# Linear attention beside softmax attention on one core: A's Q and K are copied out of PSUM before phi is made, and the engines' orders are planned anew

## The chip, the core and the metric

The kernel runs on one core of a Trainium2 chip. The core has five engines with a queue of instructions each: TensorE (PE, with its weight loads shown apart as PEld), VectorE (DVE), ScalarE (ACT), GpSimd (POOL) and SyncE (SP), which here only issues DMAs. An engine works its queue in order; where an instruction needs another engine's result it waits for a semaphore, and all that stands behind it on that engine waits too. The metric is the device time of one execution in microseconds (us).

## The reference

Two attention blocks of the same shape are computed on separate inputs and set side by side. S is 2048, D is 512, 32 heads of 16; inputs are bfloat16.

```python
def A(x, wqkv, wo):                      # linear attention
    q, k, v = heads(x @ wqkv)
    phi = lambda t: where(t > 0, t + 1, exp(t)) + 1e-6
    pq, pk = phi(q), phi(k)
    kv = einsum("bhsd,bhse->bhde", pk, v)
    z = sum over s of pk
    o = (pq @ kv) / (pq @ z + 1e-6)
    return merge(o) @ wo

def B(x, wqkv, wo):                      # softmax attention
    q, k, v = heads(x @ wqkv)
    p = softmax(q @ k^T * 16 ** -0.5)
    return merge(p @ v) @ wo

return concatenate([A, B], axis=-1)
```

## The kernel before

B is the large part. It is cut into 32 units: four groups of eight heads, four chunks of 512 query positions, and a parity (even or odd heads of the group). A unit has 64 score blocks of 128 keys x 512 queries, so there are 2048 blocks. A block is a matmul of `QT` and `KM` (line 862), an exponential, and a matmul with the values `VV` into the accumulator `pPV` (line 1106).

The exponential is made in one of two ways:

- **The ACT path.** PE writes three or two blocks at once into one of the score buffers `pS` (1536 or 1024 columns, in turn), and ACT makes exp of them in one instruction (`PT`, line 1031). Such a block has one value matmul.
- **The DVE path.** PE writes one block into one of the two banks of `pD`; DVE turns it into the bits of an approximate exponential (`DI`, line 943); POOL adds two constants to two blocks' bits at once (line 967), which gives two shifted copies. Such a block has three value matmuls.

All other products of the kernel go through the same two banks of `pD` (`DBANK`) while the score buffers are in use: B's projections, a check of the scores' size, and all of A. The A jobs are, in order: `akv_job` (for each of four column groups and eight pairs of token tiles: K and V of two tiles side by side in one bank), `akvsum_job` (phi(K)^T V), and then for each of four chunks of positions `aq_job` (Q, one bank of 512 columns, for each of four column groups), `aden_job`, `anum_job` and `omm_job`.

phi is made of three steps, written in `phi_stages`: exp on ACT into `EA` (line 692), then min with 1 plus 1e-6 on DVE in `EA` (line 693), then max(x, 0) + `EA` on DVE into `KNa` or `PQT` (line 695). The first and third read the `pD` bank, so the bank of a K/V job is held through exp, both DVE steps and V's copy to `VNa` (line 707).

The order of each engine's instructions is decided when the program is built. A planner keeps a clock per engine (`T`) and costs per operation, picks at each step one of the instructions that could start next by start time and priority, and records it with its waits in `Sched`. A job is a list of stages `(engine, cost, function)`; `rel` is the stage after which its bank is free. The table `POLICY` has one row of planner settings for each 8 us of planned time (`SEG`): priorities, thresholds, a random seed. `TEND` spreads the due times of the A and B jobs, and `DEND` is the number of blocks at the end of the last unit that are left to the ACT path alone.

An entry "PORT" in the list of what an operation writes is a token between DVE and POOL: the POOL shift and POOL's share of a unit's end name it, and so do those DVE instructions that read and write SBUF in a fast form. Through it each waits for the other by semaphores.

```python
push(eng, end + lat, 0 if i + 1 <= self.rel and self.bank else min(self.prio, 2), dur, ...)
```

is how the next stage of a job is queued: stages up to the bank's release go with the highest priority.

Of the kernel before, what the change touches and what calls it, by code (L numbers as in the profile page):

```python
# [232 lines left out]
def bass_concat_heads__linear_attn_block__softmax_full_mha__prompt_kernel(nc, A_x, A_wqkv, A_wo, B_x, B_wqkv, B_wo, out):  # L233
# [15 lines left out]
    DEND = 20  # L249
    TEND = 720.0  # L250
    TRACE = None
    NAMES = ('DEFER', 'FLOW', 'DPR', 'DDEL', 'PVR', 'PVMIN', 'PVURG', 'DBL', 'DLEAD', 'DNEXT', 'ALAG', 'SLK', 'PA', 'PB', 'SEED', 'PARTS')
    SEG = 8.0
    POLICY = [
        (0.15, 3.5, 4.2, 0, 3, 4, 32, 3.0, 1.0, 16, 10.0, 0.0, 0, 0, 0, 1),
        (0.15, 3.5, 4.2, 0, 3, 5, 32, 3.0, 1.0, 16, 10.0, 0.0, 0, 0, 201, 1),
        (0.15, 3.5, 4.2, 0.2, 3, 4, 20, 3.0, 1.0, 16, 10.0, 0.0, 0, 0, 845, 1),
        (0.35, 4.5, 2.6, 0, 3, 4, 32, 3.0, 1.0, 16, 10.0, 0.0, 0, 0, 236, 1),
        (0.35, 2.05, 4.2, 0, 3, 5, 32, 3.0, 1.0, 16, 40.0, 0.0, 0, 0, 989, 1),
        (0.15, 3.5, 4.2, 0.2, 3, 7, 20, 3.0, 1.0, 16, 10.0, 0.0, 0, 0, 845, 1),  # L260
        (0.35, 2.5, 2.6, 0, 3, 4, 32, 3.0, 1.0, 16, 10.0, 0.0, 0, 0, 24, 1),
        (0.35, 2.5, 2.6, 0, 3, 7, 32, 3.0, 1.0, 16, 10.0, 0.0, 0, 0, 222, 1),
        (0.15, 3.5, 4.2, 0.2, 3, 5, 12, 3.0, 1.0, 16, 10.0, 0.0, 0, 0, 326, 1),
        (0.15, 3.5, 3, 0, 3, 4, 32, 3.0, 0.5, 16, 10.0, 0.0, 0, 0, 0, 1),
        (0.15, 3.5, 3, 0.3, 3, 4, 32, 3.0, 0.5, 16, 10.0, 0.0, 0, 0, 0, 2),
        (0.15, 3.5, 3, 0.3, 2, 4, 32, 3.0, 0.5, 16, 10.0, 0.0, 3, 0, 0, 2),
        (0.15, 3.5, 3, 0, 3, 4, 32, 3.0, 1.0, 16, 10.0, 0.0, 0, 0, 301, 1),
        (0.15, 3.5, 4.2, 0, 3, 6, 32, 3.0, 1.0, 16, 10.0, 0.0, 0, 0, 314, 1),
        (0.5, 3.5, 3, 0, 3, 4, 20, 3.0, 1.0, 16, 10.0, 0.0, 0, 0, 95, 2),
        (0.15, 2.05, 3, 0, 3, 4, 32, 3.0, 1.0, 24, 10.0, 0.0, 0, 0, 681, 1),  # L270
        (0.5, 3.5, 3, 0, 3, 4, 20, 3.0, 1.0, 16, 10.0, 0.0, 0, 0, 430, 2),
        (0.15, 2.5, 3, 0, 3, 4, 32, 3.0, 1.0, 8, 10.0, 0.0, 0, 0, 287, 1),
        (0.15, 2.05, 3, 0, 4, 5, 32, 3.0, 1.0, 24, 10.0, 0.0, 1.5, 0, 42, 1),
        (0.5, 3.5, 3, 0, 2, 4, 20, 3.0, 1.0, 16, 10.0, 0.0, 0, 0, 430, 2),
        (0.5, 3.5, 3, 0, 2, 4, 20, 3.0, 1.0, 16, 10.0, 0.0, 0, 0, 430, 2),
        (0.15, 3.5, 3, 0, 2, 5, 24, 3.0, 1.0, 24, 10.0, 0.0, 1.5, 0, 42, 1),
        (0.15, 3.5, 4.2, 0, 3, 4, 32, 3.0, 1.0, 16, 40.0, 0.05, 0, 0, 715, 1),
        (0.35, 3.5, 3, 0, 2, 5, 24, 3.0, 0.5, 24, 10.0, 0.0, 1.5, 0, 432, 1),
        (0.15, 2.5, 4.2, 0, 3, 4, 32, 9.0, 1.0, 16, 10.0, 0.0, 0, 0, 584, 1),
        (0.15, 2.5, 4.2, 0, 3, 4, 32, 9.0, 1.0, 16, 10.0, 0.0, 0, 0, 584, 1),  # L280
        (0.35, 3.5, 3, 0, 2, 8, 24, 3.0, 0.5, 24, 10.0, 0.0, 1.5, 0, 333, 1),
        (0.15, 2.5, 4.2, 0, 3, 7, 32, 9.0, 0.5, 16, 10.0, 0.0, 0, 0, 516, 1),
        (0.15, 3.5, 4.2, 0, 3, 4, 32, 3.0, 1.0, 8, 10.0, 0.0, 0, 0, 224, 1),
        (0.15, 2.05, 4.2, 0, 3, 8, 32, 3.0, 1.0, 8, 10.0, 0.0, 0, 0, 578, 1),
        (0.25, 3.5, 4.2, 0, 3, 4, 32, 3.0, 1.0, 8, 10.0, 0.0, 0, 3, 224, 1),
        (0.15, 3.5, 4.2, 0, 2, 4, 32, 3.0, 1.0, 8, 10.0, 0.0, 0, 0, 224, 1),
        (0.25, 3.5, 4.2, 0, 3, 4, 32, 3.0, 1.0, 8, 10.0, 0.0, 0, 0.5, 893, 1),
        (0.15, 2.05, 4.2, 0, 2, 4, 32, 3.0, 1.0, 8, 10.0, 0.0, 0, 0, 224, 1),
        (0.25, 3.5, 4.2, 0, 4, 4, 32, 3.0, 1.0, 8, 10.0, 0.0, 0, 0.5, 479, 1),
        (0.15, 3.5, 4.2, 0, 3, 4, 32, 3.0, 1.0, 16, 10.0, 0.0, 0, 0, 550, 1),  # L290
        (0.25, 3.5, 4.2, 0, 4, 4, 32, 3.0, 1.0, 8, 10.0, 0.1, 3, 0.5, 215, 1),
        (0.15, 3.5, 4.2, 0.2, 3, 4, 20, 3.0, 1.0, 16, 10.0, 0.0, 0, 0, 550, 1),
        (0.15, 3.5, 4.2, 0, 3, 6, 32, 3.0, 1.0, 8, 40.0, 0.0, 0, 0, 550, 1),
        (0.15, 3.5, 2.6, 0, 3, 4, 32, 3.0, 1.0, 16, 10.0, 0.0, 1.5, 0, 414, 1),
        (0.15, 2.5, 2.6, 0, 3, 4, 32, 3.0, 1.0, 16, 10.0, 0.0, 1.5, 0, 111, 1),
        (0.15, 2.5, 3, 0, 3, 4, 32, 3.0, 0.2, 16, 10.0, 0.0, 1.5, 0, 111, 1),
        (0.15, 2.5, 2.6, 0, 4, 4, 32, 3.0, 1.0, 16, 10.0, 0.0, 1.5, 0, 111, 4),
        (0.15, 2.5, 2.6, 0, 3, 4, 32, 3.0, 1.0, 16, 20.0, 0.0, 3, 3, 368, 1),
        (0.15, 2.5, 3, 0, 2, 5, 32, 3.0, 1.0, 16, 20.0, 0.0, 3, 3, 530, 1),
        (0.15, 3.5, 4.2, 0, 2, 4, 32, 3.0, 1.0, 16, 10.0, 0.0, 0, 0, 0, 1),  # L300
        (0.15, 2.5, 2.6, 0, 3, 4, 32, 3.0, 0.5, 8, 20.0, 0.0, 3, 3, 771, 1),
        (0.15, 2.5, 3, 0.3, 2, 5, 32, 6.0, 1.0, 16, 20.0, 0.0, 3, 3, 348, 4),
        (0.15, 4.5, 4.2, 0, 2, 4, 32, 3.0, 1.0, 8, 10.0, 0.0, 0, 0, 83, 1),
        (0.35, 4.5, 4.2, 0, 4, 4, 32, 3.0, 1.0, 8, 10.0, 0.0, 0, 0, 46, 1),
        (0.15, 3.5, 4.2, 0, 3, 4, 32, 3.0, 1.0, 16, 10.0, 0.0, 0.5, 0, 3, 1),
        (0.15, 4.5, 4.2, 0, 2, 4, 32, 3.0, 1.0, 8, 10.0, 0.0, 0, 0, 73, 1),
        (0.35, 2.05, 4.2, 0, 2, 4, 32, 3.0, 1.0, 8, 10.0, 0.0, 0, 0, 46, 1),
        (0.35, 2.05, 4.2, 0, 2, 4, 32, 3.0, 1.0, 8, 10.0, 0.1, 0, 1.5, 46, 1),
        (0.15, 4.5, 4.2, 0, 2, 4, 32, 3.0, 1.0, 8, 10.0, 0.0, 0, 0, 96, 2),
        (0.15, 4.5, 2.6, 0, 2, 4, 32, 3.0, 1.0, 8, 10.0, 0.0, 0, 0, 96, 2),  # L310
        (0.35, 2.05, 4.2, 0, 2, 4, 32, 3.0, 1.0, 8, 10.0, 0.1, 0, 1.5, 511, 2),
        (0.15, 3.5, 4.2, 0, 3, 8, 16, 3.0, 1.0, 8, 10.0, 0.0, 0, 0, 0, 1),
        (0.15, 3.5, 4.2, 0, 3, 4, 32, 3.0, 1.0, 16, 40.0, 0.0, 0, 0, 673, 1),
        (0.35, 2.05, 4.2, 0, 2, 5, 32, 3.0, 1.0, 8, 10.0, 0.1, 0, 1.5, 651, 2),
        (0.15, 3.5, 4.2, 0.3, 3, 4, 16, 3.0, 1.0, 16, 20.0, 0.0, 0, 0, 0, 1),
        (0.15, 3.5, 4.2, 0, 3, 4, 32, 3.0, 1.0, 16, 20.0, 0.0, 0, 0, 330, 4),
        (0.15, 3.5, 4.2, 0.3, 3, 4, 16, 3.0, 1.0, 16, 20.0, 0.0, 0, 3, 0, 2),
        (0.15, 3.5, 4.2, 0.3, 3, 4, 16, 3.0, 1.0, 16, 20.0, 0.05, 0, 3, 0, 2),
        (0.15, 3.5, 4.2, 0, 3, 4, 32, 3.0, 1.0, 16, 20.0, 0.0, 0.5, 0, 935, 4),
        (0.15, 3.5, 4.2, 0.3, 3, 4, 32, 3.0, 0.2, 16, 20.0, 0.0, 0, 0, 0, 2),  # L320
# [1126 lines left out]
```

## Time and profile before

| | |
|---|---|
| runs shown | 714.42 us median of 3 (711.8 to 714.48) |
| profiled execution | 714.82 us; span from first to last instruction 713.1 us |
| mean granted TensorE clock | 0.994 |
| ACT busy | 691.8 us (97%) |
| PE busy | 672.3 us (94%) |
| POOL busy | 559.2 us (78%) |
| DVE busy | 537.0 us (75%) |
| exponentials on ACT (`PT`) | 591, 680.1 us busy |
| DVE conversions (`DI`) | 570, 377.2 us busy |
| POOL shifts (`DI`) | 286, 534.3 us busy |
| phi's exp on ACT (`EA`) | 48, 26.9 us busy |

The span leaves out 1.7 us that lie around it. Busy times are unions of an engine's records; durations of single records overlap on ACT, DVE and PE, since the next instruction starts before the record of the last one ends. Groups of the trace carry a line of the kernel, the engine, the operation, the tile written and the tiles read with their shapes, then the busy time and mean duration of one, and after the bar the idle time of the engine in front of them with what ended it. A row of the waits gives who waited for whom, the total, how often, and the longest. A window gives the busy time of PE, PEld, DVE, ACT and POOL in a stretch.

### The profile page before, as it was taken

Reading aid. Unit: us, or ns where it says so; the run is one execution under the profiler, and the core shown is the slowest. Engines: PE = TensorE matmul, PEld = TensorE weight load, DVE = VectorE, ACT = ScalarE, POOL = GpSimd, SP = SyncE. Lnnn points to the kernel's source line nnn. Section 1 sums busy time; section 2 is a strip of 40 time slices with the busy share of each in tenths; the row PEclk is TensorE's granted clock in tenths of the full one; section 3 lists DMA queues with packets and bytes.
Section 4 is the critical chain, followed back from the end, with each engine's and each line's share of the span. In section 5 each row is a group of like instructions: output and inputs, shape, how many; then the busy total and the mean of one; then the engine's idle time right before and its main releaser. Section 6 shows DMA issues by size and latency. Waiting matters only on the chain.

```text
span 713.1 us, 15692 instructions
## 1 busy us (share of the span) xinstructions
PE 672.3 (94%) x6691; PEld 223.7 (31%) x6691; DVE 537.0 (75%) x950; ACT 691.8 (97%) x646; POOL 559.2 (78%) x338
## 2 busy tenths in 40 slices
PE   8999999999999999999999999999999999999995
PEld 4324443333333333332222223232222222222221
DVE  4778886777767877777888778888678877878771
ACT  5999999999999999999999999999999999999995
POOL 4597577677978787877899979988678987888991
PEclk9999999999899999999999999999999999999999
DMA  9900000000000000010000000010001000011001
GB/s 215 228 1 3 2 1 10 8 8 9 1 2 1 1 2 1 3 41 13 10 23 23 17 1 1 23 24 23 9 14 25 23 16 31 10 38 30 30 17 33
DMA packets 35787, 17.32 MB, mean 24 GB/s; under 512 B 26496, under 2 KB 35200, under 8 KB 35712
## 3 DMA queue, kind: packets, MB, share of 16 engines
q1 hardware_dynamic: 34624, 15.61, 9.1%
q8 instruction: 54, 0.88, 0.5%
q10 hardware_dynamic: 1088, 0.66, 0.3%
q14 instruction: 21, 0.17, 0.1%
HBM read 4.72 MB, written 4.19 MB: 12 GB/s over the span
## 4 chain that ended last, share of the span: by engine, by line
ACT 78%; PE 12%; POOL 6%; DVE 3%; issue 1%; DVEq 0%; POOLq 0%; ACTq 0%
ACT PT L1031 76%; POOL DI L967 5%; PE pPV L1106 3%; PE pS L862 3%; ACT EA L692 2%; DVE DI L943 1%; PE pD L703 1%; PE pD L862 1%; PE pD L588 1%; PE pD L781 1%; DVE KNa L695 0%; PE pD L1151 0%; PE pD L672 0%; DVE EA L693 0%; DVE VNa L707 0%
## 5 line engine op out<-in xcount | busy, mean ns | idle before, releaser
L1031 ACT ACTIVATE PT<-pS 128x1536 f16<-128x1536 f32 (+1 forms) x591 | 680.1, 1345 | 4.8 <-PE pD L862 2.2
L967 POOL TENSOR_TENSOR DI<-DI,SHC 128x1024 int32<-128x1024 int32 (+1 forms) x286 | 534.3, 1888 | 129.3 <-DVE DI L943 86.9
L943 DVE TENSOR_SCALAR DI<-pD 128x512 int16<-128x512 f32 x570 | 377.2, 685 | 95.5 <-PE pD L862 84.9
L1106 PE MATMUL pPV<-DI,VV 128*17 128x512 f16 x1713 | 247.7, 382 | 1.8 <-DVE OT L1126 1.6
L862 PE MATMUL pS<-QT,KM 32*128 32x512 bf16 x1477 | 231.2, 386 | 19.0 <-ACT PT L1031 13.8
L1106 PE MATMUL pPV<-PT,VV 128*17 128x512 f16 x1477 | 248.0, 384 | 1.1 <-ACT PT L1031 1.0
L862 PE MATMUL pD<-QT,KM 32*128 32x512 bf16 x571 | 206.3, 386 | 7.3 <-DVE DI L943 2.5
L862 PEld LDWEIGHTS pS<-QT,KM 32*128 32x128 bf16 x1477 | 56.3, 91 | 213.2 <-ACT PT L1031 164.4
L1106 PEld LDWEIGHTS pPV<-PT,VV 128*17 128x17 bf16 x1477 | 53.0, 88 | 66.9 <-issue 51.3
L1106 PEld LDWEIGHTS pPV<-DI,VV 128*17 128x17 bf16 x1713 | 51.5, 88 | 64.5 <-issue 47.0
L862 PEld LDWEIGHTS pD<-QT,KM 32*128 32x128 bf16 x571 | 49.7, 91 | 62.7 <-DVE DI L943 34.3
L703 PE MATMUL pD<-Wa,xTa 128*128 128x128 bf16 x512 | 36.5, 223 | 0.5 <-DVE DI L943 0.4
L588 PE MATMUL pD<-xTb,Wb 128*128 128x512 bf16 x124 | 35.3, 393 | 0.4 <-DVE DI L943 0.2
L1126 DVE STREAM_TRANSPOSE OT<-pPV 128x512 f32<-128x512 f32 x32 | 22.7, 710 | 14.6 <-PE pPV L1106 14.6
L703 PEld LDWEIGHTS pD<-Wa,xTa 128*128 128x128 bf16 x512 | 29.4, 99 | 11.0 <-DVE DI L943 6.5
L692 ACT ACTIVATE EA<-pD 128x256 bf16<-128x256 f32 (+1 forms) x48 | 26.9, 560 | 0.4 <-PE pD L703 0.4
L1133 POOL TENSOR_TENSOR OT<-OT,ZR 128x256 bf16<-128x256 f32 x31 | 19.2, 619 | 8.4 <-DVE EA L693 3.7
L693 DVE TENSOR_SCALAR EA<-EA 128x256 bf16<-128x256 bf16 (+1 forms) x48 | 11.9, 248 | 15.5 <-POOL DI L967 7.2
L672 PE MATMUL pD<-Wb,xTb 128*128 128x128 bf16 x256 | 18.3, 220 | 1.6 <-DVE DI L943 0.8
L781 PE MATMUL pD<-WOa,ONT 128*128 128x512 bf16 x64 | 18.0, 383 | 0.2 <-DVE DI L943 0.2
L728 PE MATMUL pD<-xTa,Wa 128*128 128x512 bf16 x64 | 17.6, 383 | 0.3 <-DVE DI L943 0.2
L677 DVE CAST VV<-pD 128x512 bf16<-128x512 f32 x16 | 11.1, 692 | 8.0 <-PE pD L672 7.9
(94 smaller groups left out, 264.8 us busy)
## 6 DMA issues: line engine op xcount, KB each, us to landing
out_dram<-OB SPq DMA_DIRECT2D x16, 128.0 KB, 1.7
out_dram<-KNa SPq DMA_DIRECT2D x14, 128.0 KB, 1.7
Wa<-in_A_wqkv_dram SPq DMA_DIRECT2D x1, 1536.0 KB, 8.2
KM<-KR SPq DMA_DIRECT2D x96, 16.0 KB, 1.8
Wb<-in_B_wqkv_dram SPq DMA_DIRECT2D x2, 384.0 KB, 4.5
Wb<-in_B_wqkv_dram SPq DMA_DIRECT2D x1, 512.0 KB, 4.9
WOa<-in_A_wo_dram SPq DMA_DIRECT2D x1, 512.0 KB, 8.9
VNa<-in_B_wo_dram SPq DMA_DIRECT2D x1, 512.0 KB, 3.3
```

The costliest lines, as they stand in the source:

```text
L588: return e.matmul(f32v(bk), lhsT=Wb[:, cc, kind * 512 + Gp * 128:kind * 512 + Gp * 128 + 128], rhs=xTb[:, cc, sc * 512:(sc + 1) * 512], st ...
L672: return e.matmul(f32v(bk)[:, tl * 128:(tl + 1) * 128], lhsT=xTb[:, cc, t * 128:(t + 1) * 128], rhs=Wb[:, cc, 1024 + Gp * 128:1024 + Gp * ...
L692: ("act", 0.051 + n * 0.000833, f_ev("act", lambda e, bk: e.activation(EA[:, q, 0:n], f32v(bk)[:, c0:c0 + n], ACTF.Exp), [], [("EA", q)])),
L703: return e.matmul(f32v(bk)[:, 128 * x:128 * x + 128], lhsT=xTa[:, cc, (t + i_) * 128:(t + i_ + 1) * 128], rhs=Wa[:, cc, c0:c0 + 128], star ...
L781: return e.matmul(f32v(bk), lhsT=src, rhs=WO[:, hb, :], start=(hb == 0), stop=(hb == 3))
L862: return e.matmul(dst, lhsT=KM[32 * g:32 * g + 32, Gp % 2, e_, j * 128:(j + 1) * 128], rhs=QT[32 * g:32 * g + 32, Gp % 2, c * 512:(c + 1) ...
L943: sch.add("dve", lambda e: e.tensor_scalar(DI[:, buf, 0, i * 512:(i + n) * 512], DB[:, bi * 512:(bi + n) * 512], ESC, EB, op0=ALU.mult, op ...
L967: sch.add("pool", lambda e: e.tensor_tensor(DI32[:, buf, 1:3, 0:w], DI32[:, buf, 0, 0:w].unsqueeze(1).broadcast_to([128, 2, w]), SHC32[:]. ...
L1031: sch.add("act", lambda e: e.activation(PT[:, row, c0:c0 + w], SCR[sl][:, 0:w], ACTF.Exp, scale=SC), reads=skeys(sl), writes=[("PT", row, ...
L1106: sch.add("pe", lambda e, g=g, vk=vk, c0=c0, P=P, first=first, last_=last_: e.matmul(PVb[32 * g:32 * g + 17, 0:512], lhsT=VV[:, Gp % 2, vk ...
L1126: sch.add("dve", lambda e: e.transpose(OT[:, 0, :], PVb[:, 0:512]), reads=[("PV", g) for g in range(4)], writes=[("OT", 0)])
L1133: (ml, 0.65 if ml == "pool" else 0.36, f_op(ml, lambda e: e.tensor_tensor(xn[:, :, 16 * e_:16 * e_ + 16], o[:, :, 0:16], zr.unsqueeze(2).b ...
```

## The change

The bank of a K/V job is emptied by two DVE copies, K into `KNa` and V into `VNa`, and is then free (`rel=3`). That of a Q job is emptied by one copy into `PQT` (`rel=2`). phi is then made from the copy, in place: exp from `KNa` or `PQT` into `EA` on ACT, max(x, 0) + 1e-6 in place on DVE, then min(`EA`, 1) + x in place on DVE. The last step has two SBUF inputs now and carries the "PORT" token as well; it did not before.

The rest is the planner. Three settings are added to each row (`WJ`: wait for a second free `pD` bank before a score fill; `AQ`: put a phi exp off; `LW`: DVE instructions with the token that are older than this go first, and POOL is given nothing meanwhile). Stages on ACT behind a bank's release get priority 0. A late A job stops the DVE path only when it could start. `DEND` goes from 20 to 12, `TEND` from 720 to 695, and the table of settings is another one. So the order of all engines changes from the first microseconds on. The sum of blocks on the ACT path goes from 1477 to 1467, that on the DVE path from 571 to 581.

```diff
-    DEND = 20
-    TEND = 720.0
+    DEND = 12
+    TEND = 695.0
...
-    NAMES = ('DEFER', 'FLOW', 'DPR', 'DDEL', 'PVR', 'PVMIN', 'PVURG', 'DBL', 'DLEAD', 'DNEXT', 'ALAG', 'SLK', 'PA', 'PB', 'SEED', 'PARTS')
+    NAMES = ('DEFER', 'FLOW', 'DPR', 'DDEL', 'PVR', 'PVMIN', 'PVURG', 'DBL', 'DLEAD', 'DNEXT', 'ALAG', 'SLK', 'PA', 'PB', 'SEED', 'PARTS', 'WJ', 'AQ', 'LW')
...
-        (0.15, 3.5, 4.2, 0, 3, 5, 32, 3.0, 1.0, 16, 10.0, 0.0, 0, 0, 201, 1),
-        (0.15, 3.5, 4.2, 0.2, 3, 4, 20, 3.0, 1.0, 16, 10.0, 0.0, 0, 0, 845, 1),
...
+        (0.15, 3.5, 4.2, 0, 3, 4, 32, 3.0, 1.0, 16, 10.0, 0.0, 0, 0, 0, 1, 0.0, 0.0, 2.0),
+        (0.15, 3.5, 4.2, 0, 3, 4, 32, 3.0, 1.0, 16, 10.0, 0.0, 0, 0, 303, 1, 0.0, 2.0, 2.0),
...
-                        push(eng, end + lat, 0 if i + 1 <= self.rel and self.bank else min(self.prio, 2), dur,
+                        push(eng, end + lat + (P["AQ"] if eng == "act" and i >= self.rel and self.bank else 0.0), (0 if i + 1 <= self.rel and self.bank else 0 if eng == "act" else min(self.prio, 2)), dur,
...
-        def phi_stages(c0, n, out_ap, okeys):
+        def phi_stages(n, t_ap, keys):
...
-                ("act", 0.051 + n * 0.000833, f_ev("act", lambda e, bk: e.activation(EA[:, q, 0:n], f32v(bk)[:, c0:c0 + n], ACTF.Exp), [], [("EA", q)])),
-                ("dve", 0.067 + n * 0.00026, f_op("dve", lambda e: e.tensor_scalar(EA[:, q, 0:n], EA[:, q, 0:n], 1.0, 1e-6, op0=ALU.min, op1=ALU.add),
-                                               [("EA", q)], [("EA", q), "PORT"])),
-                ("dve", 0.067 + n * 0.00105, f_ev("dve", lambda e, bk: e.scalar_tensor_tensor(out_ap, f32v(bk)[:, c0:c0 + n], 0.0, EA[:, q, 0:n],
-                                                                                          op0=ALU.max, op1=ALU.add), [("EA", q)], okeys))]
+                ("act", 0.051 + n * 0.000833, f_op("act", lambda e: e.activation(EA[:, q, 0:n], t_ap, ACTF.Exp), list(keys), [("EA", q)])),
+                ("dve", 0.067 + n * 0.00026, f_op("dve", lambda e: e.tensor_scalar(t_ap, t_ap, 0.0, 1e-6, op0=ALU.max, op1=ALU.add), [], list(keys) + ["PORT"])),
+                ("dve", 0.067 + n * 0.00105, f_op("dve", lambda e: e.scalar_tensor_tensor(t_ap, EA[:, q, 0:n], 1.0, t_ap, op0=ALU.min, op1=ALU.add),
+                                                [("EA", q)], list(keys) + ["PORT"]))]
...
-            st += phi_stages(0, 256, KNa[:, t:t + 2, :].rearrange("p t n -> p (t n)"), [("KNa", t), ("KNa", t + 1)])
+            st.append(("dve", 0.34, f_ev("dve", lambda e, bk: e.tensor_copy(KNa[:, t:t + 2, :], f32v(bk, 256).rearrange("p (b n) -> p b n", n=128)),
+                                         [], [("KNa", t), ("KNa", t + 1)])))
             st.append(("dve", 0.34, f_ev("dve", lambda e, bk: e.tensor_copy(VNa[:, t:t + 2, 0:128], f32v(bk)[:, 256:512].rearrange("p (b n) -> p b n", n=128)),
...
+            st += phi_stages(256, KNa[:, t:t + 2, :].rearrange("p t n -> p (t n)"), [("KNa", t), ("KNa", t + 1)])
             return Job(st, [("xTa", t), ("xTa", t + 1)] + ([("akv", bq - 1)] if bq else []),
-                       [(5, ("ak", bq, t))], **kw)
+                       [(6, ("ak", bq, t))], rel=3, **kw)
...
-            st += phi_stages(0, 512, PQT[:, 0, bq, :], [("PQT", 0, bq)])
+            st.append(("dve", 0.6, f_ev("dve", lambda e, bk: e.tensor_copy(PQT[:, 0, bq, :], f32v(bk)), [], [("PQT", 0, bq)])))
+            st += phi_stages(512, PQT[:, 0, bq, :], [("PQT", 0, bq)])
...
-                       [(4, ("aq", sc, bq))], **kw)
+                       [(5, ("aq", sc, bq))], rel=2, **kw)
...
-            if (ajobs and at > ajobs[0].ready + P["ALAG"]) or (bjobs and at > bjobs[0].ready + P["ALAG"] and bjobs[0].start_time() is not None):
+            if (ajobs and at > ajobs[0].ready + P["ALAG"] and ajobs[0].start_time() is not None) or (bjobs and at > bjobs[0].ready + P["ALAG"] and bjobs[0].start_time() is not None):
...
+            aged = [c_ for c_ in cands["dve"] if c_[5] and max(T["dve"], T["pool"]) > c_[0] + P["LW"]]
             for eng in T:
                 best = None
+                if eng == "pool" and aged:
+                    continue
...
+            if fa is not None and lim is not None and P["WJ"] and d_open():
+                have = sum(x is not None and x <= fa[0] + 0.05 for x in jfree[0:2])
+                nxt = [x for x in jfree[0:2] if x is not None and fa[0] + 0.05 < x <= min(fa[0] + P["WJ"], lim)]
+                if have < min(2, 4 - ABL[nfill[0] % 2]) and nxt:
+                    fa = (min(nxt),) + fa[1:]
```

## The prediction

> **What bounds the kernel now.** I read the page's first and fourth parts (busy time, the chain that ended last), then ScalarE's (ACT's) own waits, then its timeline, and last the groups kept apart by shape, for the prices.
>
> ```profile
> PE 672.3 (94%) x6691; PEld 223.7 (31%) x6691; DVE 537.0 (75%) x950; ACT 691.8 (97%) x646; POOL 559.2 (78%) x338
> ...
> ACT 78%; PE 12%; POOL 6%; DVE 3%; issue 1%; DVEq 0%; POOLq 0%; ACTq 0%
> ```
>
> ACT is busy 97% of 713.1 us and carries 78% of the chain. PE's 94% is no rival bound: PE's weight loads wait 164.4 us in total for `PT`, that is, for ACT to hand score banks back.
>
> ```profile
> ACT KNa L556 <- PE pD L808: 3.9, 1, 3.9
> ACT QT L1165 <- PE pD L588: 3.7, 1, 3.7
> ...
> ACT PT L1031 <- PE pD L862: 2.2, 5, 1.0
> ...
> ACT EA L692 <- PE pD L703: 0.4, 1, 0.4
> ```
>
> The two largest waits are start and end (before 12.18 us, after 703.86 us). Between them ACT visibly waits only about 5 us; 2.2 us stand against "PE pD", score matmuls that queue on PE behind a matmul into the two shared `pD` banks. So time after = ACT's start + its work + its waits + a tail of 9.2 us (703.86 to 713.1), unless another engine takes over.
>
> ```profile
> 12.18 51.39 ACT L1031 ACTIVATE PT<-pS 128x1536 f16<-128x1536 f32 x45 [0.80 <-PE pS L862]
> 63.27 0.58 ACT L692 ACTIVATE EA<-pD 128x256 bf16<-128x256 f32 x1
> 63.54 14.86 ACT L1031 ACTIVATE PT<-pS 128x1024 f16<-128x1024 f32 x13
> ...
> 315.13 0.65 ACT L692 ACTIVATE EA<-pD 128x512 bf16<-128x512 f32 x1
> 315.61 15.99 ACT L1031 ACTIVATE PT<-pS 128x1024 f16<-128x1024 f32 x14
> ...
> 518.44 66.65 ACT L1031 ACTIVATE PT<-pS 128x1024 f16<-128x1024 f32 x59
> 584.91 0.67 ACT L692 ACTIVATE EA<-pD 128x512 bf16<-128x512 f32 x1
> ```
>
> Records overlap on ACT, so the price of an instruction is the step from its start to the next start: `EA` of 256 columns 63.27 to 63.54 = 0.27 us, of 512 columns 315.13 to 315.61 = 0.48 us. A quiet stretch gives the exponentials: 518.44 to 584.91 is 66.47 us for 59, so 2.253 us for a pair (1536 + 1024 columns, five blocks). Against that pace I count what ACT loses. Whole: 691.7 us less 32 x 0.27 and 16 x 0.48 (16.3) leaves 675.4; 591 exponentials are 295.5 pairs, 665.8 us; lost 9.6 us. In A's K/V stage alone: from the `EA` at 106.79 to that at 198.51 the timeline has 75 exponentials and 11 `EA`, 91.7 - 84.5 - 3.0 = 4.2 us lost; from there to 315.13 it has 98 and 15, 116.6 - 110.4 - 4.0 = 2.2 us. So 6.4 of the 9.6 us are lost in the 208 us in which A's K and V use the `pD` banks.
>
> ```profile
> 100.00:200.00 100.00, 95.11 (x980) 35.06 (x981) 73.55 (x148) 97.29 (x95) 74.44 (x45) 0.97 0.03 7
> ...
> 500.00:600.00 100.00, 95.72 (x880) 26.48 (x879) 75.98 (x124) 100.00 (x93) 79.89 (x46) 1.00 0.08 21
> ```
>
> The windows agree (fourth figure is ACT): 97.29 in a K/V stretch, 100.00 later.
>
> **The change part by part, against the profiled execution's 714.82 us** (span 713.1 plus 1.7; the median of the runs shown, 714.42, is 0.4 below it, inside their spread of 2.7).
>
> *1. Split of the 2048 score blocks.* In the new order ACT has 293 exponentials of 1536 and 294 of 1024 columns (before 295 and 296), VectorE (DVE) and POOL the other 581 blocks (before 571). Four exponentials less are two pairs: -4.5 us on the bound. The ten blocks cost others: about six DVE units of 0.685 us (six 512-column conversions less, eight of 1024 columns more, +5.7 us in all), five shifts on POOL at 1.891 (+9.5), 20 value matmuls net on PE, shared among four column groups. All of them have 40 to 176 us of idle time.
>
> *2. `EA` reads SBUF.* Same 48 instructions, same sizes, but the source is `KNa` or `PQT` instead of `pD`. The nearest rows are the present ones, 0.27 and 0.48 us, which would make this 0. Here a rule speaks against the change: the Trainium skill, "Perfetto Trace Analysis", section "Optimizing Scalar/DVE Operations", puts ScalarE's overhead per instruction at about 93 ns on SBUF against 51 ns on PSUM. The trace's 0.48 less 0.27 is 0.21 us for 256 columns, which leaves 0.06 of overhead, near the 51; no long ACT instruction in this trace reads SBUF, so the other half is not shown. By the trace 0, by the rule an estimate of 48 x 0.042 = +2.0 us. I take +2.0: same operation, only the source differs.
>
> *3. Copies on DVE.* Prices:
>
> ```profile
> L692 ACT ACTIVATE EA<-pD 128x256 bf16<-128x256 f32 x32 | 15.5, 485 | 0.4 <-PE pD L703 0.4
> ...
> L695 DVE SCALAR_TENSOR_TENSOR KNa<-pD,EA 128x256 bf16<-128x256 f32 x32 | 13.6, 424 | 1.0
> ...
> L707 DVE CAST VNa<-pD 128x256 bf16<-128x256 f32 x32 | 13.3, 417 | 0.0
> ...
> L597 DVE CAST QT<-pD 128x512 bf16<-128x512 f32 x15 | 10.3, 686 | 4.9 <-PE pD L588 4.8
> ...
> L693 DVE TENSOR_SCALAR EA<-EA 128x256 bf16<-128x256 bf16 x32 | 7.2, 226 | 11.6 <-POOL DI L967 4.8 <-ACT EA L692 2.9 <-POOL OT L1133 2.3
> ```
>
> 32 copies like L707 and 16 like L597: 13.3 + 16 x 0.686 = +24.3 us on DVE. The tensor_scalar keeps its size; the scalar_tensor_tensor keeps its row (0.424 and 0.691) or gets a little cheaper, since both inputs are now in SBUF: 0. DVE goes from 537 to about 567 us. Cover: its 176 us of idle time. Price for the end: 0 while the cover holds.
>
> *4. The port token.* The code's "PORT" key makes POOL and some DVE instructions wait for each other. Before: 48 tensor_scalars and 32 `VV` ones. Now the 48 scalar_tensor_tensors too, and in the new order a POOL instruction stands between the two phi instructions in 41 of 48 cases.
>
> ```profile
> POOL DI L967 <- DVE EA L693: 25.3, 29, 4.4
> POOL DI L967 <- DVE VV L681: 15.4, 16, 2.4
> ...
> DVE EA L693 <- POOL DI L967: 7.2, 12, 1.4
> ```
>
> With the smaller rows of the kind (POOL's `OT` 3.7 and 1.5; DVE on `OT` 2.8, `VV` 1.6) 80 such instructions cost POOL 45.9 us, 0.57 each, and DVE 11.6 us, 0.15 each. 48 more: POOL +27, DVE +7. With the five shifts POOL needs 37 of its 154 idle us. Price for the end 0, but the slack of two engines shrinks together; without cover, POOL's excess goes to the end one for one through value matmuls. Were the token absent, the records would not tell whether two SBUF inputs and POOL slow each other.
>
> *5. The bank.* Before, a `pD` bank of a K/V job is held from its matmuls through `EA` (behind an exponential of up to 1.33 us on ACT), the tensor_scalar (behind a POOL instruction, up to 1.4 us of wait), the scalar_tensor_tensor (0.42) and V's copy (0.42). Now through two copies, 0.84 us; for Q one copy, 0.69. Score matmuls no longer queue on PE behind a matmul that waits for such a bank. Bounds: all 6.4 us lost in the K/V stage come back (-6.4), or the planner fills the banks at once with its ten extra blocks and nothing does (0), or the denser PE queue loses as much again (+6.4). Outside that stage ACT loses (9.6 - 6.4) / 483 us, at which pace 208 us would lose 1.4; I take most of the way to it, -4.5.
>
> *6. A new wait.* `EA` now waits for DVE's copy, not for PE. ACT works in order, so a late copy stops every exponential behind it, then PE's score matmuls that wait for ACT's banks. Followed back through its waits, the copy depends on the activation four places before its `EA` in 36 of 48 cases (before, the matmul on the one three before in 46): one exponential more, 0.9 to 1.3 us, to place a copy of 0.42 or 0.69. Bounds: 0, and 48 x 0.69 = 33 us if every copy is a whole copy late. Nearest row: ACT's wait for `EA`'s matmul, 0.4 us in total. I take +0.8, twice that.
>
> *7. Orders, tail, queues.* `DEND` 12 instead of 20 lets the DVE path into the last blocks; DVE was idle 10.83 us before its last transpose, so that is cover, but POOL's last shift now stands two or three exponentials before the end instead of five. 0, bounds -1 and +2 (one shift). SP keeps its 96 `KM` issues, 16 transposes and its stores in slightly other order; DMA share is 0.01 to 0.08 in the windows, price 0. A `KM` transfer that came late would hold both score paths.
>
> Sum: -4.5 + 2.0 - 4.5 + 0.8 = -6.2; 714.8 - 6.2 = **708.6 us**.
>
> **Rivals.**
> - *ACT waits for copies (slower).* Place: ACT's queue in front of the 48 `EA`. When DVE waits for POOL it is 0.6 us a time (7.2 / 12), more than a copy. At 0.3 us mean per `EA` it is 14.4 us, and with no bank relief 714.8 - 4.5 + 2.0 + 14.4 = 727; at 0.2 it is 722. It outweighs parts 1, 2 and 5 from 7.0 / 48 = 0.15 us mean. For it: 48 more token waits sit in the queue that makes the copies. Against it: 176 us of DVE idle time and the extra exponential of distance.
> - *Nothing comes back from the banks.* Parts 1 and 2 alone: 712.3; with 1 to 2 us of copy waits, 714. No change.
> - *The orders win more.* All 9.6 us of ACT loss go: 714.8 - 2.5 - 9.6 = 702.7; if `EA` from SBUF costs nothing as well, 700.7. For it: the pace of 518 to 585 us held across 59 exponentials. Against it: A's jobs still need DVE in the K/V stage.
> - *POOL or PE becomes the bound.* Needs POOL to lose over 117 us more than I count; small.
>
> **How the numbers follow.** About 0.5% (3.6 us) is what a measurement of this kernel can tell from no change, so faster means under 710.8, slower over 718.0. The forecast has 0.45, its own range 704 to 713, of which 0.40 is faster and 0.05 same. More from the orders: 0.20, faster. Nothing back: 0.13, same. Waits for copies: 0.22, slower. Together 0.60, 0.18, 0.22. The range 700.5 to 720 leaves out the strong half of the slower case and what lies beyond the best one.
>
> **What would show it.** Part 1: ACT's exponential group falls by four. Part 2: the step from an `EA` start to the next is 0.31 and 0.52 rather than 0.27 and 0.48. Part 5: ACT's busy share of 100 to 200 us over 99%, and "PE pD" gone from its waits. Part 6: ACT's wait "EA <- DVE" under 2 us; over 8 us, the slower rival. Part 4: POOL's wait for phi instructions near 55 us. Wrong altogether: ACT busy below 95% in the middle windows, or POOL near 100%.

## The result and the profile after

| | before | after |
|---|---|---|
| median, us | 714.44 (711.8 to 714.48, 4 runs) | 706.23 (704.43 to 706.54, 4 runs) |
| ratio | | 0.9889 [0.9861, 0.9917] |
| profiled execution, us | 714.82 | 704.43 |
| span, us; mean granted clock | 713.1; 0.994 | 702.7; 0.999 |
| first exponential starts, last ends, us | 12.18, 703.86 | 9.46, 693.67 |

The changed kernel is 1.1% faster; 708.6 had been forecast. The page's busy times and the shares of the chain, after:

```profile
PE 661.4 (94%) x6710; PEld 220.2 (31%) x6710; DVE 560.2 (80%) x1000; ACT 686.7 (98%) x642; POOL 568.9 (81%) x343
...
ACT 83%; PE 6%; POOL 6%; DVE 3%; issue 1%; POOLq 0%; DVEq 0%; ACTq 0%
```

ACT is still the bound, and more so (78% of the chain before). DVE and POOL work more, about as counted, and stay nearly as far off the path as before. ACT's own waits (total, times, longest):

```profile
ACT KNa L555 <- PE pD L809: 3.4, 1, 3.4
...
ACT QT L1166 <- PE pD L587: 2.0, 1, 2.0
...
ACT PT L1032 <- PE pD L863: 1.3, 4, 0.5
ACT PT L1032 <- PE pS L863: 0.6, 1, 0.6
```

The first two are again the end and the start. No line says that `EA` waits for DVE. The "PE pD" line has fallen from 2.2 to 1.3 us, not to nothing. The steps of `EA`, from two stretches of ACT's timeline:

```profile
62.86 0.45 ACT L691 ACTIVATE EA<-KNa 128x256 bf16<-128x256 bf16 x1
63.16 1.06 ACT L1032 ACTIVATE PT<-pS 128x1024 f16<-128x1024 f32 x1
...
312.56 0.81 ACT L691 ACTIVATE EA<-PQT 128x512 bf16<-128x512 bf16 x1
313.08 1.64 ACT L1032 ACTIVATE PT<-pS 128x1536 f16<-128x1536 f32 x1
```

From start to next start `EA` now takes 0.30 and 0.52 us. In most of the 48 cases the two sizes step 0.305 and 0.519, where reading PSUM they stepped 0.263 and 0.476. The windows (length, then busy time of PE, PEld, DVE, ACT, POOL, then clock, DMA share, GB/s):

```profile
100.00:200.00 100.00, 94.75 (x1022) 35.10 (x1021) 81.26 (x164) 99.38 (x98) 75.69 (x44) 1.00 0.03 7
200.00:300.00 100.00, 96.18 (x1066) 37.26 (x1062) 82.46 (x168) 99.56 (x98) 84.23 (x49) 1.00 0.02 6
500.00:600.00 100.00, 94.93 (x897) 26.49 (x897) 81.86 (x136) 100.00 (x92) 86.98 (x51) 1.00 0.08 20
```

ACT's share of 100 to 200 us rose from 97.29 to 99.38. But another figure moved with it: the clock, from 0.97 to 1.00. The prediction shows that 0.97 and does not read it.

The same bookkeeping as in the prediction, on the trace after: 684.2 us from first to last exponential; less 32 x 0.305 and 16 x 0.52 (18.1) and 293.5 pairs x 2.253 (661.3), 4.8 us are lost, where 9.6 were (how far these levels can be trusted is said under "Why the prediction was right"). In the K/V stage (from the `EA` at 103.10 to that at 312.56: 177 exponentials and 26 `EA`) 209.5 - 199.4 - 7.9 = 2.1 us, where 6.4 were lost.

### A stretch at half clock in the profile before

Windows of one microsecond of the profile before, over the place where its clock figure fell:

```profile
191.00:192.00 1.00, 0.92 (x5) 0.28 (x4) 1.00 (x3) 1.00 (x2) 0.96 (x2) 0.97 0.00 0
192.00:193.00 1.00, 1.00 (x9) 0.22 (x12) 0.68 (x3) 1.00 (x2) 1.00 (x1) 0.50 0.00 0
...
195.00:196.00 1.00, 1.00 (x7) 0.17 (x4) 0.58 (x2) 0.38 (x1) 0.97 (x2) 0.50 0.00 0
...
198.00:199.00 1.00, 1.00 (x11) 0.42 (x12) 0.07 (x1) 0.54 (x3) 0.00 (x0) 0.62 0.03 8
199.00:200.00 1.00, 1.00 (x19) 0.24 (x15) 0.96 (x4) 1.00 (x1) 0.76 (x2) 1.00 0.00 0
```

For nearly 7 us TensorE ran at half clock. From PE's timeline, the same 16 matmuls just before it and in it, and from ACT's timeline what it meant there:

```profile
186.65 1.07 PE L703 MATMUL pD<-Wa,xTa 128*128 128x128 bf16 x16
...
196.59 1.89 PE L703 MATMUL pD<-Wa,xTa 128*128 128x128 bf16 x16
```

```profile
195.62 2.52 ACT L1031 ACTIVATE PT<-pS 128x1024 f16<-128x1024 f32 x2 [1.01 <-PE pD L862]
198.51 0.38 ACT L692 ACTIVATE EA<-pD 128x256 bf16<-128x256 f32 x1 [0.36 <-PE pD L703]
```

Both waits read "<-PE pD", as if a bank had been held; PE was busy all the while and slow. By the steps from the `EA` at 188.18 to that at 203.66 (11 exponentials and two `EA`) ACT lost 2.4 us there. The profile after has no such stretch between its first and last exponential. So 2.4 of the 6.4 us that the prediction put down to held banks lie in this one. Nor did a held bank lead up to it: of the 0.56 us for which PE was idle in the 4 us ahead, 0.35 were a wait for ACT's score banks, 0.12 one for V's copy and 0.09 one for a conversion.

The other executions hint at how common it is: each reports its mean clock, though not where the clock fell. A stretch of 7 us at half clock takes 0.5 x 7 / 713 = 0.005 off the mean. But in all 14 profiles the clock also falls to half behind the last matmul, for 0.1 to 5.3 us of the span, which slows no matmul and takes up to 0.004 off. E12's profile has a mean of 0.996 from that alone (PE's busy time is the first after the length):

```profile
698.00:704.00 6.00, 0.00 (x0) 0.00 (x0) 0.37 (x1) 0.60 (x1) 0.00 (x0) 0.55 0.32 97
```

So the groups below count stretches only roughly.

| mean granted clock | executions of the kernel before, beside the experiments | median, us |
|---|---|---|
| 0.996 and 0.997 | 6 of 42 | 711.1 |
| 0.990 to 0.994 | 20 | 713.2 |
| 0.985 to 0.988 | 16 | 715.1 |

About 2 us go with each step of the clock. The changed kernel stood at 0.996 to 1.000 in all of its 9 executions (median 705.9). Against 713.7, the median of the 42, it gains 7.8 us, of which by this reading about 713.7 - 711.1 = 2.6 go with half-clock stretches that the new order doesn't have. That is inferred from means; the profile shows one stretch of one execution. The other 5.2 are close to what the bookkeeping gives without them: 4.5 for four exponentials less, 2.4 for other waits (9.6 - 2.4 - 4.8), less 1.8 for dearer `EA` (2.0 by the finer steps) makes 5.1.

### The profile page after: what moved, and what is told of

The parts are those of the page before. It is cut to its first block, busy times and chain, and to the rows that moved or that the text cites. A ratio compares the mean times of both kernels' runs of the same rounds, so it can differ in the third digit from the quotient of the medians.

```text
span 702.7 us, 15761 instructions
## 1 busy us (share of the span) xinstructions
PE 661.4 (94%) x6710; PEld 220.2 (31%) x6710; DVE 560.2 (80%) x1000; ACT 686.7 (98%) x642; POOL 568.9 (81%) x343
## 4 chain that ended last, share of the span: by engine, by line
ACT 83%; PE 6%; POOL 6%; DVE 3%; issue 1%; POOLq 0%; DVEq 0%; ACTq 0%
ACT PT L1032 81%; POOL DI L968 6%; ACT EA L691 2%; PE pPV L1107 2%; PE pS L863 2%; DVE DI L944 1%; PE pD L587 1%; PE pD L863 0%; PE pD L1152 0%; DVE KNa L693 0%; PE pD L701 0%; DVE VV L680 0%; DVE GR L657 0%; DVE KNa L692 0%; DVE OT L1127 0%
## 5 line engine op out<-in xcount | busy, mean ns | idle before, releaser
L1032 ACT ACTIVATE PT<-pS 128x1536 f16<-128x1536 f32 x587 | 673.7, 1360 | 2.5 <-PE pD L863 1.3
L968 POOL TENSOR_TENSOR DI<-DI,SHC 128x1024 int32<-128x1024 int32 x291 | 544.3, 1890 | 114.6 <-DVE DI L944 49.6
L944 DVE TENSOR_SCALAR DI<-pD 128x512 int16<-128x512 f32 (+1 forms) x572 | 382.6, 692 | 70.5 <-PE pD L863 63.2
L1107 PE MATMUL pPV<-DI,VV 128*17 128x512 f16 x1743 | 243.5, 382 | 1.8 <-POOL DI L968 0.9
L1107 PE MATMUL pPV<-PT,VV 128*17 128x512 f16 x1467 | 241.1, 382 | 1.2 <-ACT PT L1032 1.0
L1107 PEld LDWEIGHTS pPV<-PT,VV 128*17 128x17 bf16 x1467 | 51.5, 88 | 63.5 <-issue 47.0
L782 PE MATMUL pD<-WOa,ONT 128*128 128x512 bf16 x64 | 18.3, 383 | 0.2 <-issue 0.2
L704 DVE CAST KNa<-pD 128x256 bf16<-128x256 f32 x32 | 13.4, 418 | 6.3 <-PE pD L701 6.1
L693 DVE SCALAR_TENSOR_TENSOR KNa<-EA,KNa 128x256 bf16<-128x256 bf16 x32 | 13.4, 420 | 4.1 <-POOL DI L968 3.5
```

Of the source, the lines that this page charges most:

```text
L782: return e.matmul(f32v(bk), lhsT=src, rhs=WO[:, hb, :], start=(hb == 0), stop=(hb == 3))
L944: sch.add("dve", lambda e: e.tensor_scalar(DI[:, buf, 0, i * 512:(i + n) * 512], DB[:, bi * 512:(bi + n) * 512], ESC, EB, op0=ALU.mult, op ...
L968: sch.add("pool", lambda e: e.tensor_tensor(DI32[:, buf, 1:3, 0:w], DI32[:, buf, 0, 0:w].unsqueeze(1).broadcast_to([128, 2, w]), SHC32[:]. ...
L1032: sch.add("act", lambda e: e.activation(PT[:, row, c0:c0 + w], SCR[sl][:, 0:w], ACTF.Exp, scale=SC), reads=skeys(sl), writes=[("PT", row, ...
L1107: sch.add("pe", lambda e, g=g, vk=vk, c0=c0, P=P, first=first, last_=last_: e.matmul(PVb[32 * g:32 * g + 17, 0:512], lhsT=VV[:, Gp % 2, vk ...
```

## The experiments

"First row" means that the first row of the kernel's own table is used for every segment, so that no settings are searched. "New planner" includes the new `DEND` and `TEND`. "Lost" is the bookkeeping above, on the profiled execution. "Half clock" is the time in windows of half a microsecond below 0.9, between first and last exponential. Each ratio is to the kernel before, run beside it; not all experiments ran on one chip, so across them ratios are safer than medians.

| | median, us | ratio | lost, us | half clock, us |
|---|---|---|---|---|
| E1 before, first row | 734.78 | 1.0298 [1.0248, 1.0347] | 18.3 | 12.0 |
| E2 after, first row | 733.63 | 1.0283 [1.0233, 1.0333] | 23.0 | 10.5 |
| E3 old phi, new planner, first row | 738.91 | 1.0379 [1.0315, 1.0443] | 20.9 | 0 |
| E4 E2 with banks held | 778.58 | 1.0919 [1.0869, 1.097] | 57.6 | 39.5 |
| E5 after, last phi step without token | 722.78 | 1.0128 [1.0091, 1.0165] | 19.5 | 15.5 |
| E6 after, copies made twice | 720.86 | 1.0103 [1.0063, 1.0143] | 20.2 | 11.0 |
| E7 old phi, after's planner and table | 737.45 | 1.0329 [1.029, 1.0368] | 30.5 | 7.0 |
| E8 old phi, new planner, own table | 707.67 | 0.9913 [0.9896, 0.993] | 5.3 | 0 |
| E9 copies, own table | 711.10 | 0.9968 [0.9953, 0.9983] | 10.7 | 3.5 |
| E10 after again | 705.62 | 0.9886 [0.9866, 0.9906] | 4.7 | 0 |
| E11 E9 with `EA` priced | 705.95 | 0.9891 [0.9871, 0.9912] | 8.5 | 4.0 |
| E12 E11 searched longer | 706.05 | 0.9907 [0.9883, 0.993] | 7.8 | 0 |

**E1 to E4: the parts without a search.** E1 and E2 are the two kernels with the first row everywhere:

```diff
     POLICY = (
         (0.15, 3.5, 4.2, 0, 3, 4, 32, 3.0, 1.0, 16, 10.0, 0.0, 0, 0, 0, 1, 0.0, 0.0, 2.0),
-        (0.15, 3.5, 4.2, 0, 3, 4, 32, 3.0, 1.0, 16, 10.0, 0.0, 0, 0, 303, 1, 0.0, 2.0, 2.0),
+        (0.15, 3.5, 4.2, 0, 3, 4, 32, 3.0, 1.0, 16, 10.0, 0.0, 0, 0, 0, 1, 0.0, 0.0, 2.0),
...
```

> The kernel before with its first settings row in all segments: no searched orders, old data flow, old planner rules. If the orders found by the search carry most of this kernel's speed, it is 15 to 30 us slower than the kernel before (730 to 745); if the data flow alone sets the time, within 5 us of 714.

> The changed kernel with its first row everywhere: copies first, new planner rules, no searched orders. If the shorter bank hold by itself brings the gain, it is 6 to 10 us faster than the other flat kernel (old data flow and old rules). If the hold only gives the search room, the two flat kernels are within 3 us of each other.

E3 is E2 with `phi_stages`, `akv_job` and `aq_job` as before. E4 is E2 with the copies, but each bank held to the job's last stage:

```diff
-                       [(6, ("ak", bq, t))], rel=3, **kw)
+                       [(6, ("ak", bq, t))], **kw)
...
-                       [(5, ("aq", sc, bq))], rel=2, **kw)
+                       [(5, ("aq", sc, bq))], **kw)
```

> New planner rules, DEND and TEND, first row everywhere, but phi made from the PSUM bank as before. Against the flat kernel with copies this is the data flow alone. Bank theory: 5 to 8 us slower than that one, with ACT's waits on pD larger in the K/V stage. Orders theory: within 2 us of it.

> Copies first and first row everywhere, but the planner gives the bank out only after the last phi step (later than in the kernel before, since the copies come on top). Only the hold is changed. Bank theory: 15 us or more slower than the flat kernel with copies, with more blocks left to ACT in the K/V stage. If the hold doesn't matter: same within 2 us.

With no search the whole change is worth nothing: E1 and E2 agree within their intervals. With the new planner for both, the copies (E2) are 5.3 us faster than the old phi (E3), about 3.5 if only executions with a clock of 0.995 or more are set side by side. That is the size that the bank theory expected, but not by its way: ACT's waits are not smaller with the copies (17.1 us of idle time between first and last exponential in E2, 14.8 in E3). What differs is the split, 562 blocks on the DVE path in E2 and 547 in E3, worth 6.8 us at 2.253 for five. The new planner alone (E3 against E1) is no gain. That the release matters once the copies are there is plain from E4, 45 us slower than E2, with 537 blocks on the DVE path. Its ACT waits, and then those of E2 for a copy:

```profile
ACT PT L1045 <- PE pD L876: 26.5, 26, 5.6
ACT EA L704 <- DVE KNa L717: 17.8, 8, 9.0
```

```profile
ACT EA L704 <- DVE KNa L717: 0.9, 3, 0.4
ACT EA L704 <- DVE PQT L744: 0.8, 1, 0.8
```

This is the wait that the slower rival was built on, with a copy up to 9.0 us late. It is large when the banks are held, and small but not absent when they are freed: 1.7 us in E2, 0.9 each in E9 and E12, none in the changed kernel.

**E7 to E9: whose gain is it?** E7 puts the old phi under the changed kernel's planner and table. For E8 and E9 I searched a table for each data flow, segment by segment in the planner's own model from the first row, with the same effort (4 partial orders kept, 14 trials each).

```diff
-            st += phi_stages(256, KNa[:, t:t + 2, :].rearrange("p t n -> p (t n)"), [("KNa", t), ("KNa", t + 1)])
+            st += phi_stages(0, 256, KNa[:, t:t + 2, :].rearrange("p t n -> p (t n)"), [("KNa", t), ("KNa", t + 1)])
...
```

> The changed kernel's planner, table of settings, DEND and TEND, with phi made from the PSUM bank as before. Data flow theory: about 5 us slower than the changed kernel. Theory that the table belongs to the data flow it was searched for: 25 us or more slower (over 730), near the flat kernels, since the orders drift apart from the first A job on.

> New planner rules, DEND and TEND; phi from the PSUM bank as before; a table of settings that I searched for this data flow from the flat row (beam of 4, 56 tries a segment). 572 blocks on the DVE path by its order. Theory that the data flow makes the gain: 712 to 716, no faster than the kernel before. Theory that the search and its rules make most of it: 708 to 712.

> The same rules and the same search effort for copies first. 585 blocks on the DVE path. Data flow theory: 6 to 8 us faster than the searched old flow. Search theory: at most 3 us faster than it, 707 to 710.

E7 is 31 us slower than the changed kernel: a table belongs to the data flow it was searched for. E8 is the run that decides. It holds its banks through phi like the kernel before, and yet loses only 5.3 us. From a K/V job's last matmul to its bank's release the traces have 2.77 us before, 2.54 in E8 and 1.10 after the change (means of 32 jobs). Its ACT waits and windows:

```profile
ACT PT L1038 <- PE pS L869: 1.2, 3, 0.6
ACT PT L1038 <- PE pD L869: 1.0, 3, 0.5
```

```profile
100.00:200.00 100.00, 93.48 (x996) 35.41 (x1001) 73.83 (x148) 99.10 (x99) 71.61 (x42) 1.00 0.03 7
200.00:300.00 100.00, 96.32 (x1059) 38.30 (x1059) 76.27 (x150) 99.65 (x99) 79.50 (x46) 1.00 0.03 8
```

The K/V stage is as full as after the change, at full clock, in all six executions 0.997 to 0.999. So banks held through phi don't force the loss: an order searched for that flow avoids it too. E8 stays 2.05 us behind E10 on the same chip. The intervals of the ratios overlap, but the executions don't: 707.2 to 708.1 against 705.0 to 706.4. What it lacks is the split of the blocks: 572 on the DVE path, not 581. E9, with the copies and the same short search, has 585 there but came out 3.4 us slower than E8, against both expectations. At equal effort of search, then, the old data flow was ahead. E10 has the same data flow as E9 and a better table, worth 5.5 us; how long that table was searched for is not known, and the old flow was not searched longer.

**E10 to E12: the price of `EA` in the planner.** E10 repeats the changed kernel. E11 searches the new flow again with the overhead of `EA` at its measured size (6 partial orders, 22 trials); E12 searches longer (8, 29).

```diff
-                ("act", 0.051 + n * 0.000833, f_op("act", lambda e: e.activation(EA[:, q, 0:n], t_ap, ACTF.Exp), list(keys), [("EA", q)])),
+                ("act", 0.093 + n * 0.000833, f_op("act", lambda e: e.activation(EA[:, q, 0:n], t_ap, ACTF.Exp), list(keys), [("EA", q)])),
```

> The changed kernel itself, on the same chip as the two searched ones, to hold them against: 704 to 707.

> Copies first, with the planner told the measured price of EA from SBUF (0.042 us more for each of the 48) and a longer search (beam of 6, 132 tries a segment). If the planner's wrong price costs stalls beyond the 2 us themselves, it is faster than the searched kernel without it by over 2 us and may reach 705; if not, the same within 2 us.

> Copies first, EA from SBUF priced at its measured cost, and a longer search still (beam of 8, 232 tries a segment). If a right price and better orders are what is left to win, it is faster than the changed kernel (705.6 on the last chip) by 1 to 4 us: 702 to 705. If not, 705 to 708.

Both tie with the changed kernel and don't beat it. Whether E11's 5 us over E9 come from the right price or from the longer search was not separated. They put 587 and 589 blocks on the DVE path and lose 3 to 4 us more in waits: what the split gives, the waits take.

**E5 and E6: tokens and DVE time, in an unchanged order.** E5 keeps the changed kernel's order and drops only the token of phi's last step, which has two SBUF inputs:

```diff
+        def f_np(lane, fn, reads=(), writes=()):
+            op = lambda bk: sch.add(lane, fn, reads=reads, writes=[w for w in writes if w != "PORT"])
+            op.keys = writes
+            return op
...
-                ("dve", 0.067 + n * 0.00105, f_op("dve", lambda e: e.scalar_tensor_tensor(t_ap, EA[:, q, 0:n], 1.0, t_ap, op0=ALU.min, op1=ALU.add),
+                ("dve", 0.067 + n * 0.00105, f_np("dve", lambda e: e.scalar_tensor_tensor(t_ap, EA[:, q, 0:n], 1.0, t_ap, op0=ALU.min, op1=ALU.add),
```

> The changed kernel in exactly its order, with the 48 scalar_tensor_tensors free of the PORT token (no semaphore between them and POOL in either direction). Theory that the token is covered: same as the changed kernel within 1 us (706), POOL's waits for DVE's third phi step (32 us) and DVE's waits for POOL in front of it (6 us) gone or moved to other rows. Theory that the token costs: 2 to 4 us faster. If the hardware makes the two wait for each other anyhow, POOL's shift or the scalar_tensor_tensor shows longer durations than 1.89 and 0.42 us.

It got 16.6 us slower than the changed kernel (17 by the ratios), which neither theory had, though the longer durations had been named as possible. The groups, in the changed kernel and then in E5:

```profile
L693 DVE SCALAR_TENSOR_TENSOR KNa<-EA,KNa 128x256 bf16<-128x256 bf16 x32 | 13.4, 420 | 4.1 <-POOL DI L968 3.5
...
L693 DVE SCALAR_TENSOR_TENSOR PQT<-EA,PQT 128x512 bf16<-128x512 bf16 x16 | 11.0, 684 | 2.7 <-POOL DI L968 2.6
```

```profile
L698 DVE SCALAR_TENSOR_TENSOR KNa<-EA,KNa 128x256 bf16<-128x256 bf16 x32 | 26.7, 835 | 0.1
L698 DVE SCALAR_TENSOR_TENSOR PQT<-EA,PQT 128x512 bf16<-128x512 bf16 x16 | 20.8, 1301 | 0.0
```

The semaphore waits are gone, and the instruction itself now waits for POOL. Of the 48, 25 are lengthened by more than 0.1 us; each of these starts during a POOL instruction and ends a fixed time behind that one's end, 0.28 us at 256 columns and 0.55 at 512. It works the other way too: POOL's shifts last up to 2.34 us in E5 and 1.90 with the token. One such case followed through E5's timelines, DVE first, then PE, ACT, and a window:

```profile
180.42 2.07 DVE L698 SCALAR_TENSOR_TENSOR KNa<-EA,KNa 128x256 bf16<-128x256 bf16 x1
182.41 1.27 DVE L949 TENSOR_SCALAR DI<-pD 128x512 int16<-128x512 f32 x2
```

```profile
183.14 1.68 PE L719 MATMUL pD<-VNa,KNa 128*128 128x129 bf16 x16 [1.30 <-DVE DI L949]
```

```profile
185.40 1.02 ACT L1037 ACTIVATE PT<-pS 128x1024 f16<-128x1024 f32 x1 [1.90 <-PE pD L868]
```

```profile
184.00:185.00 1.00, 1.00 (x11) 0.65 (x9) 0.15 (x1) 0.00 (x0) 1.00 (x2) 0.50 0.00 0
```

The stalled step makes the next two conversions late, PE waits 1.30 us for the `pD` bank they hold, its clock then drops to half for 3.5 us, and ACT waits 1.90 us. There are four such stretches in E5. Of the 13.8 us for which ACT is idle between first and last exponential (1.9 after the change), 7.6 lie in or at the edge of them.

E6 makes each K and Q copy twice, in the same order, 24.4 us more work for DVE:

```diff
+        def f_ev2(lane, fn, reads=(), writes=()):
+            def two(bk):
+                for _ in range(2):
+                    sch.add(lane, lambda e: fn(e, bk), reads=[bk[3]] + list(reads), writes=writes)
+            return two
...
-            st.append(("dve", 0.6, f_ev("dve", lambda e, bk: e.tensor_copy(PQT[:, 0, bq, :], f32v(bk)), [], [("PQT", 0, bq)])))
+            st.append(("dve", 0.6, f_ev2("dve", lambda e, bk: e.tensor_copy(PQT[:, 0, bq, :], f32v(bk)), [], [("PQT", 0, bq)])))
```

> The changed kernel in exactly its order, with each copy of K and of Q done twice by DVE (24 us more of DVE work that the orders don't allow for; K's and Q's bank and EA wait for the second). Slower rival of the prediction: ACT waits for DVE in front of EA, 48 x 0.2 to 0.4 us, so 10 us or more slower than 706 and a wait EA <- DVE of that size. Theory that a cover of one exponential stands before EA: EA waits under 3 us in total, and the time rises by at most 5 us.

It got 14.6 us slower (15 by the ratios), 60% of the added work, though DVE is idle for 142 us of the changed kernel's span. ACT's waits in E6:

```profile
ACT PT L1038 <- PE pD L869: 5.0, 12, 0.9
ACT PT L1038 <- PE pS L869: 3.6, 8, 0.7
...
ACT EA L697 <- DVE PQT L737: 3.1, 4, 1.0
```

The time is what the slower rival expected, the wait is not: of the 12.9 us for which ACT is idle, only 3.4 are `EA` waiting for a copy, and 8.6 are waits for PE. The likely way is that of E5, a bank that DVE frees late holding up PE and ACT's score banks behind it; it was not followed case by case here. Two stretches at half clock (11 us) hold 3.5 of the 12.9 us.

## Why the prediction was right, and where not

The sum was -6.2 us; the profiled executions differ by 10.4. Of these 2.7 lie ahead of the first exponential, 7.5 between first and last, 0.2 behind. The 7.5 answer to the sum, the 2.7 are not the change's (last section). The total came within 2.4 us of the measured median, but partly by luck: the term for the bank, 4.5 us, was met in size by something else.

The bookkeeping's levels are too low, its differences are not. The pace of 2.253 us a pair comes from a stretch that has 0.8 us of waits in it, and whose 59 exponentials are 30 of 1024 columns and 29 of 1536. Over the whole trace the commonest steps are 0.904 and 1.330 us, 2.234 for a pair. By them ACT loses 15.3 us before and 10.4 after, of which 8.0 and 4.0 in the K/V stage. So that stage held about half of the loss before, not two thirds.

*1. Split of the blocks: right.* ACT makes four exponentials less, 587 for 591, worth the 4.5 us. POOL's busy time rose by 9.7 us, where five shifts were counted at 9.5. Of the two figures for DVE the sum, 5.7, was right (5.4 measured); "six units of 0.685" would be 4.1.

*2. `EA` from SBUF: right, and the rule beat the trace before.* The steps are 0.042 and 0.043 us longer, so 48 cost 2.0 us. Taking the rows of the trace before would have given 0.

*3. Copies on DVE: the prices right, the cover only half understood.* The rows, from the changed kernel's groups:

```profile
L704 DVE CAST KNa<-pD 128x256 bf16<-128x256 f32 x32 | 13.4, 418 | 6.3 <-PE pD L701 6.1
...
L731 DVE CAST PQT<-pD 128x512 bf16<-128x512 f32 x16 | 11.0, 687 | 2.0 <-PE pD L728 1.8
```

24.4 us, for 24.3 counted, and none of it shows on ACT. But "0 while the cover holds", with 176 us of idle DVE time as the cover, was the wrong reason. E6 adds the same 24.4 us again beside 142 us of idle time, and 14.6 come out. What covers the copies is an order that was made with them in it.

*4. The token: right at 0, and POOL's wait sized well.*

```profile
POOL DI L968 <- DVE KNa L693: 17.1, 22, 2.0
POOL DI L968 <- DVE PQT L693: 15.0, 14, 1.8
...
POOL DI L968 <- DVE KNa L692: 11.3, 19, 2.5
POOL DI L968 <- DVE PQT L692: 9.4, 12, 2.2
```

These are 52.8 us; POOL's `OT` instructions add 6.4, so 59 for the 55 named. What the prediction left open, whether two SBUF inputs and POOL slow each other without the token, E5 answers: they do, and here, in an order made with the token, dropping it costs 16.6 us.

*5. The bank: the size right by luck, the cause not.* The hold did become shorter, 1.10 us for 2.77, and ACT lost 4.3 us less in the K/V stage, for 4.5 forecast. But 2.4 of that was a stretch at half clock in the profile before, which stood in a shown row as 0.97 and was read as a held bank. The rest is not shown to be the copies' doing either: E8 holds the banks for 2.54 us and runs the stage as full. What brings the waits down in E8 is the order (or its new rules; the two were not parted). Where the copies do help, in the first row (E2 against E3), it is by more blocks on the DVE path and not by fewer waits.

*6. A new wait: 0 for 0.8.* No `EA` of the changed kernel waits for a copy.

*7. Tail: 0.2 us shorter, for 0.* SP and POOL's queue showed nothing.

**The rivals.** Waits for copies, the slower one, came true in size only in E4, where the bank is held. Where DVE is loaded beyond its plan (E6) the kernel does get slower, mostly by another path. Nothing back from the banks is refuted as a sum, since ACT's waits did fall; that the freed banks made them fall is not shown. That the orders win more is nearest to what was seen: in E8 a search on the old data flow with the new rules gets to within about 2 us of the changed kernel. What is left for the copies is that more blocks can go over the DVE path (581 to 589 in the searched orders with copies, 571 and 572 in those without), and 2.0 of the 4.5 us that ten blocks bring go back to dearer `EA`.

Left open: a search for the old flow under the old rules was not run, so E8's gain is not divided between rules and search; nor was one for the old flow as long as E11's, so the last 2 us are not shown to be out of its reach. Nor is it settled what sets off a half-clock stretch.

## What to carry to other kernels

Read the clock figure of a window before blaming a wait in it: a wait for a busy PE at clock 0.50 looks like a wait for a held bank, and an execution's mean clock hints at how many such stretches it had, once the fall at its end is taken off. Idle time of an engine is no cover for work that its order was not planned with: 142 us of it did not hide 24 in E6. To judge a change of data flow under a planner, search an order for both flows; under one table, E7 and the changed kernel differ by 31 us where the searched ones differ by 2.

## What was not expected of the hardware

**Half clock without a long pause.** The windows fall to exactly 0.50, for about 3.5 or 7 us, once for 13.6 (E4). PE's idle time in the 4 us ahead doesn't decide it. In E5 each of the four stretches follows 1.1 to 1.5 us of it, most of that in one piece. The profile before had 0.56, and one stretch of E4, from 304.19, only 0.16, while E12 had 1.56 and no fall behind it:

```profile
187.93:191.93 4.00, 3.44 (x29) 0.90 (x25) 3.30 (x7) 4.00 (x5) 3.55 (x3) 1.00 0.00 0
...
300.19:304.19 4.00, 3.84 (x30) 1.13 (x30) 3.54 (x7) 4.00 (x4) 4.00 (x3) 1.00 0.12 29
...
111.00:115.00 4.00, 2.44 (x23) 0.64 (x23) 3.54 (x5) 3.27 (x4) 2.64 (x2) 1.00 0.00 0
115.00:120.00 5.00, 4.90 (x67) 1.94 (x59) 3.67 (x8) 5.00 (x5) 2.95 (x2) 1.00 0.09 20
```

The Trainium skill, "TensorE: Matmul & The Clock Gate", section "What's actually happening", has the two rates and a free-running window of 3.4 us, of which the lengths are multiples; its section "🎯 Why this matters for your kernels" warns of idle gaps over about 3 us. No single gap ahead of a fall was that long here: the longest was 2.3 us, in E4.

**DVE blocked by POOL.** In E5 an instruction of 0.42 us took up to 2.07 beside a shift of 1.9 us on POOL. With one input in PSUM, as before the change, the same operation ran without a token at 424 ns in the mean, 427 at the longest, though 33 of those 48 (both sizes) overlapped a POOL instruction. "SBUF — State Buffer", section "🔬 SBUF: two separate sides", has VectorE instructions with two SBUF inputs and GpSimd share a pair of ports under an exclusive lock; E5 agrees.

**A start that comes in two speeds.** PE's first four projection matmuls, in the profile before and after:

```profile
7.15 1.89 PE L588 MATMUL pS<-xTb,Wb 128*128 128x512 bf16 x4 [0.69 <-ACT xTb L556]
```

```profile
6.33 1.04 PE L587 MATMUL pS<-xTb,Wb 128*128 128x512 bf16 x4 [0.73 <-ACT xTb L555]
```

Of the 14 profiles three, before, E4 and E11, show the slow pace and the others the fast one, so it does not go with the change. The first exponential starts at 12.0 to 12.2 us in the three and at 9.5 to 10.4 in the others. In E10, whose first of these matmuls starts at 7.16 as in the profile before, it comes 1.9 us earlier; so 1.9 of the 2.7 us are the pace, and 0.8 an earlier start. The clock figure reads 1.00 there in both.
